# An attention and SwiGLU kernel: five of seven output products split once more, gate and value weights streamed

## The chip, the cores and the metric

The kernel runs on one core of a Trainium2 chip. The metric is the device time of one execution in microseconds. Four compute engines work beside each other: TensorE (PE, matrix products into PSUM), VectorE (DVE), ScalarE (ACT) and GpSimd (POOL); SyncE (SP) issues the transfers (DMAs) between HBM and the on-chip memory SBUF. Each engine runs its own instructions in a fixed order and waits on semaphores for the others.

## The reference

Attention over 8 batches of 8 heads, 576 tokens, head width 64, where scores more than `tau` below their row's maximum are dropped; then a SwiGLU feed-forward block over the 4608 tokens, all in float32:

```python
scores = scale * np.matmul(q, k.transpose(0, 1, 3, 2))
thresh = np.max(scores, axis=-1, keepdims=True) - tau
scores = np.where(scores >= thresh, scores, -1000000000.0)
...
attn = attn / (np.sum(attn, axis=-1, keepdims=True) + 1e-09)
attn_out = np.matmul(attn, v)
...
g = x @ w_gate                      # x: 4608 x 512, w_gate: 512 x 1536
silu = g * (1.0 / (1.0 + np.exp(-g)))
val = x @ w_val
return (silu * val @ w_out)         # w_out: 1536 x 512
```

## The kernel before

**The work.** A batch has four head pairs ("segments"), and each pair five slots: four tiles of 128 query tokens and a half tile of 64. So a batch has slots 0 to 19 (`kk`), and the half tiles are slots 4, 9, 14 and 19. A slot computes the scores of its tile (`slot_scores`, line 1155; PSUM tiles `sc`, two of them, each for 64 tokens and two heads), then the softmax (`slot_rest`, line 1181): row maxima on DVE, exponents on ACT, masks with row sums on DVE, an exchange of sums on ACT, the scaling by the reciprocal sum, half of it on GpSimd (line 1237) and half on ACT (line 1240), and a transpose on DVE (line 1241). One slot into the next segment, in slots 1, 6, 11 and 16, `attend` (line 1246) multiplies the segment's turned tiles by the values. It needs the transposes of all five slots.

**The feed-forward block of the batch before** runs in the same slots, for the first 512 tokens of each batch (a chunk `c`, here `c = b - 1`); the last 64 tokens of all batches form a ninth chunk. The products are by Winograd's form of Strassen's scheme: a product of 2 x 2 blocks by 7 block products instead of 8, with sums of blocks before and after.
- Gate and value: six groups of 256 columns per chunk, each with 7 products p1 to p7 of four matmuls 128x256 (class `Group`, line 878). Four of the seven weight operands lie in SBUF for good (`wgv`; one block is replaced by a difference, line 823). The three others are sums, stored once in HBM (`sums_hbm`) and loaded per group into a ring of two places, 768 KB each (`load_sums`, line 829).
- Output: class `Outputs` (line 1028) takes 256 tokens at a time, and so twice 7 products, each of six matmuls 128x256. Its results are added up in the tile `ob` by ACT copies and DVE additions with one operand in PSUM, and shipped by DMAs (`ship`, line 1079).

**What sets the order.** A class `Plan` collects jobs for DVE, ACT, POOL and SP, each with an estimated duration, the jobs it depends on and a rank, and puts them into each engine's order by when they can start. PE's order is written by hand: after a slot's scores come so many products of gate and value by the table `GV`, and so many output products by `CH` (`block_part`, line 1351):

```python
GV = {2: 4, 3: 3, 4: 3, 5: 4, 6: 1, 7: 4, 8: 3, 9: 3, 10: 3, 11: 2, 12: 4, 13: 4, 14: 3}
CH = {16: 1, 17: 3, 18: 2, 19: 2, 0: 3, 1: 1}
```

The output products of chunk c thus run from slot 15 to slot 1 of the next batch. After the last batch comes a tail (`tail[0] = True`): the last two chunks alone, without attention, with all sums of blocks on DVE.

Of the kernel before, what the change touches and what calls it, by code (L numbers as in the profile page):

```python
# [10 lines left out]
F32 = mybir.dt.float32  # L11
# [7 lines left out]
class Job:  # L19


    def __init__(self, eng, took, fn, rank, lag):
        self.eng, self.took, self.fn, self.rank, self.lag = eng, took, fn, rank, lag
        self.waits, self.ready, self.end, self.then = 0, 0.0, None, []


class Plan:
# [7 lines left out]
    def __init__(self):  # L35
        self.t = 0.0
        self.free = dict.fromkeys(("DVE", "ACT", "POOL", "SP"), 0.0)
        self.open = {e: [] for e in self.free}

    def job(self, eng, took, fn, *deps, rank=1, lag=0.0):  # L40
        j = Job(eng, took, fn, rank, lag)
        for d in deps:
            if isinstance(d, Job) and d.end is None:
                d.then.append(j)
                j.waits += 1
            elif d is not None:
                j.ready = max(j.ready, self.after(d, eng) if isinstance(d, Job) else d + self.HOP)
        if not j.waits:
            self.open[eng].append(j)
        return j  # L50
# [20 lines left out]
    def step(self):  # L71
        start, e, n = self.peek()
        j = self.open[e].pop(n)
        start = max(start, j.ready)
        j.fn()
        self.free[e] = start + j.took
        j.end = start + j.took + j.lag
        for k in j.then:
            k.waits -= 1
            k.ready = max(k.ready, self.after(j, k.eng))  # L80
            if not k.waits:
                self.open[k.eng].append(k)
# [26 lines left out]
def kernel(  # L109
# [64 lines left out]
    wgv = const.tile([P, 2, NCC, DFF], F32, name="wgv")  # L174
    wo = const.tile([P, 2, NF, DM2], F32, name="wo")
    extra = const.tile([P, 3 * WS], F32, name="extra")
    ring = const.tile([P, 2, 3 * HW], F32, name="ring")
# [4 lines left out]
    ob = const.tile([P, 2, DM], F32, name="ob")  # L182
    sums_hbm = hbm.tile([NF2, P, 3 * HW], F32, name="sums_hbm")
    last_hbm = hbm.tile([P, NCC, B * (S - SM)], F32, name="last_hbm")

    rall = ring.rearrange("p s n -> p (s n)")
# [46 lines left out]
    los = deque([extra[:, 4 * S + 2 * TW:], rall[:, 4 * S:], ob.rearrange("p i n -> p (i n)")[:, 0:TW]])  # L233
# [529 lines left out]

    def ring_part(s, n):
        return ring[:, s, n * HW:(n + 1) * HW].rearrange("p (k f) -> p k f", k=2)

# [47 lines left out]
    def weight_sums(g, place, *deps):  # L814
        t1, t2, t4 = (place[:, n * HW:(n + 1) * HW].rearrange("p (k f) -> p k f", k=2) for n in range(3))
        w11, w12, w21, w22 = pair_cols(wval, 0, g), pair_cols(wgat, 0, g), pair_cols(wval, 1, g), pair_cols(wgat, 1, g)
        j = job("POOL", 1.3, pool_tt(t1, w12, w11, ALU.subtract), *deps, rank=3)
        j = job("POOL", 1.3, pool_tt(t2, w22, t1, ALU.subtract), j, rank=3)
        j = job("POOL", 1.3, pool_tt(t4, w21, t2, ALU.subtract), j, rank=3)
        stores[g] = job("SP", 0.1, lambda: nc.sync.dma_start(out=sums_hbm[g], in_=place), j, lag=4.0)  # L820
        summed_g[g] = j
# [5 lines left out]
    loads = {}  # L827

    def load_sums(c, g, *deps):
        loads[c, g] = job("SP", 0.1, lambda: nc.sync.dma_start(out=ring[:, g % 2], in_=sums_hbm[g]), stores[g], *deps, lag=4.0)  # L830
# [47 lines left out]
    class Group:  # L878


        def __init__(self, c, g):
            self.c, self.g = c, g
            self.b = None

# [9 lines left out]
        def ring_w(self, n):  # L894
            return ring_part(self.g % 2, n)

# [5 lines left out]
        def p1(self, early=True):  # L902
            self.a = take("pa")
            self.m1 = self.mul(self.a, pair_cols(wval, 0, self.g), x_block(self.c, 0, 0), True, *self.a.deps, *ready_x[self.c][0])
            self.a.bank.full = True
            if early:
                self.take_b()

        def p5(self):
            self.take_b()  # L910
            self.e = take("pe")
            m = self.mul(self.e, self.ring_w(0), xs[0], True, loads[self.c, self.g], *ready_x[self.c][1], *self.e.deps)
            self.e.bank.full = True
            s, old = turn_of(s_bufs)
            self.s = s
            self.s5 = job("ACT", 0.55, lambda: nc.scalar.activation(s.ap, self.e.rows(), AF.Copy, scale=0.5), m, *old, rank=0)  # L916

        def p2(self):
            u, self.u1_old = turn_of(u_bufs)
            self.u1_buf = u  # L920
            if self.b is None:
                self.s1 = job("ACT", 0.55, lambda: nc.scalar.copy(u.ap, self.a.rows()), self.m1, *self.u1_old, rank=0)
                self.u1_old = []
            m = self.mul(self.a, pair_cols(wval, 1, self.g), x_block(self.c, 0, 1), False, self.cb if self.b else self.s1)
            self.m2 = m

        def p6(self):
            u = self.u1_buf
            if self.b:
                m = self.mul(self.b, self.ring_w(1), xs[1], False, self.cb, *ready_x[self.c][2])  # L930
            else:
                b = self.b = take("pb")
                m = self.mul(b, self.ring_w(1), xs[1], True, *ready_x[self.c][2], *b.deps)
                m = job("DVE", 0.7, lambda: nc.vector.tensor_tensor(out=b.rows(), in0=b.rows(), in1=u.ap, op=ALU.add),
                        m, self.s1, rank=0)
                b.bank.full = True
            self.u1 = job("ACT", 0.55, lambda: nc.scalar.activation(u.ap, self.b.rows(), AF.Copy, scale=0.5), m, *self.u1_old, rank=0)

# [14 lines left out]
        def p3(self):  # L953
            m = self.mul(self.e, pair_cols(wgat, 1, self.g), xs[2], False, self.s5, *ready_x[self.c][4])
            u = self.u1_buf
            g1 = job("DVE", 0.7, lambda: nc.vector.scalar_tensor_tensor(out=u.ap, in0=self.e.rows(), scalar=0.5, in1=u.ap, op0=ALU.mult,
                                                                        op1=ALU.add), m, self.u1, rank=0 if self.g == NF2 - 1 else 1)
            self.e.read_by(g1)
            self.e.done(True)
            self.finish(0, u, g1, self.a, self.m2)  # L960

        def p7(self):
            m = self.mul(self.b, pair_cols(wgat, 0, self.g), x_block(self.c, 1, 0), False, self.u1, parts[self.g], *ready_x[self.c][3])
# [7 lines left out]
        def p4(self):  # L971
            m = self.mul(self.b, self.ring_w(2), x_block(self.c, 1, 1), False, self.u2)
            self.finish(1, self.u2_buf, self.g2, self.b, m)
            if self.g + 2 < NF2:
                load_sums(self.c, self.g + 2, m)
# [52 lines left out]
    class Outputs:  # L1028
# [53 lines left out]
        def products(self):  # L1082
# [11 lines left out]
            def three():  # L1094
# [3 lines left out]
                z["s4"] = []  # L1098
# [27 lines left out]
    def outputs(c):  # L1126
# [10 lines left out]
        def run():  # L1137
            n, s, fn = steps.pop(0)
            fn()
            if s == 4:  # L1140
                mark = plan.t
                if n == 0:
                    units[1].half_sums(mark)
                elif c < B:
                    load_sums(c + 1, 0, mark)
                    if c == 0:
                        load_sums(1, 1, stores[NF2 - 1])
            return bool(steps)

        return first, run  # L1150

# [29 lines left out]
    def slot_rest(seg, t, pss, marks):  # L1181
# [53 lines left out]
        for x in range(m):  # L1235
            if x % 2 and t < NT:
# [51 lines left out]
    def prepare_next(i, later_than):  # L1288
# [10 lines left out]
        fj = job("SP", 0.8, fetch, later_than, lag=3.5)  # L1299
# [10 lines left out]
    def prepare_v(seg, *deps):  # L1310
        seg["vj"] = job("SP", 0.4, lambda: load_v(seg), *deps, lag=3.5)
# [9 lines left out]
    def gates_and_values(c):  # L1321

        old = None
        for g in range(NF2):
# [3 lines left out]
            if old is not None:  # L1328
                old.p4()
                yield  # L1330
            for fn in (new.p5, new.p2, new.p6, new.p3, new.p7):
                fn()
                yield
            old = new
        state["last_product"] = old.p4
# [10 lines left out]
    GV = {2: 4, 3: 3, 4: 3, 5: 4, 6: 1, 7: 4, 8: 3, 9: 3, 10: 3, 11: 2, 12: 4, 13: 4, 14: 3}  # L1346
    CH = {16: 1, 17: 3, 18: 2, 19: 2, 0: 3, 1: 1}
    PLAIN = {5: 2, 6: 0, 10: 2, 11: 0}
    CH0 = {14: 1, 15: 3, 16: 0, 17: 2, 18: 2, 19: 2, 20: 3, 21: 1}

    def block_part(b, kk):
# [13 lines left out]
        if kk in GV:  # L1365
            if kk == 2:
                state["gv"] = gates_and_values(c)
            gv_steps(GV[kk])
            if kk == 14:
                next(state["gv"], None)  # L1370
                first, state["run"] = outputs(c)
                first.half_sums()
        elif kk == 15:
            out_steps(1)
            state["last_product"]()
            load_sums(c + 1, 1, plan.t)
            out_steps(1)
        elif state["run"]:
            out_steps(CH.get(kk, 0))

    own = xall[:, 3 * XW:]
    WS = {8: (0, own), 9: (1, ring[:, 1]), 11: (2, own), 13: (3, ring[:, 1]), 15: (4, ring[:, 1]), 17: (5, ring[:, 1])}
    for n, seg in enumerate(halved):
        i = seg["i"]
        for x, t in enumerate(seg["tiles"]):
# [19 lines left out]
            slot_rest(seg, t, pss, marks)  # L1405
# [10 lines left out]
            if 18 <= s < 18 + 2 * NF2 and s % 2 == 0:  # L1416
                g = (s - 18) // 2
                weight_part(g, summed_g[g], plan.t)

    tail[0] = True  # L1420
    out_steps(3)
    attend(halved[-1])
    spare = []
# [14 lines left out]
    for c in (B - 1, B):  # L1438
        for _ in gates_and_values(c):
            pass  # L1440
        first, state["run"] = outputs(c)
        first.half_sums()
        out_steps(1)
        state["last_product"]()
        if c < B:
            load_sums(B, 1, plan.t)
# [42 lines left out]
```

## Time and profile before

| | |
|---|---|
| median of 3 runs | 1439.74 us (1439.49 to 1439.96) |
| the profiled execution | 1440.44 us, of which the span from first to last instruction is 1438.7 |
| granted TensorE clock | 0.998 of full speed |
| one batch (attend of slot 11 to the next) | 154.5 us |
| scores 128x288 exponent on ACT / mask on DVE | 495 / 510 ns |
| scaling of a tile on ACT / on POOL | 529 / 1012 ns |
| row maxima on DVE, per score tile | 747 ns |
| sum of 128x512 on POOL | 1275 ns |
| loads of weight sums | 48 of 768 KB, 4.5 us from issue to landing |

"PE" are matmuls and "PEld" the weight loads that run beside them. A float32 matmul leaves two records, so record counts are twice the number of matmuls. In the rows of groups the columns are the line, the engine, the operation, output and inputs with their tile names, the number of records, the busy time in us, and the mean of one in ns. A busy engine is not one that sets the time: that is seen from which wait ends last.

### The profile page before, as it was taken

How to read it: one execution, taken by the hardware profiler on the slowest of the kernel's cores; microseconds unless marked ns; L12 is line 12 of the kernel's file. 1: busy time of each engine (PE TensorE's matmuls, PEld its weight loads, DVE VectorE, ACT ScalarE, POOL GpSimd, SP SyncE). 2: the span in 40 equal slices, each digit the busy share in tenths (PEclk: the TensorE clock that was granted, in tenths of full speed). 3: DMA queues.
4: the chain of work that ended last, by engine and by line, in shares of the span. 5: the costliest groups of instructions: out<-in, count | busy, mean ns of one | idle time of the engine just before them, and what ended most of it. 6: DMA issues, size and time to landing. Idle time of an engine off the chain costs nothing.

```text
span 1438.7 us, 31145 instructions
## 1 busy us (share of the span) xinstructions
PE 1400.7 (97%) x11496; PEld 1078.7 (75%) x11496; DVE 1061.6 (74%) x3045; ACT 794.0 (55%) x2170; POOL 697.8 (49%) x686
## 2 busy tenths in 40 slices
PE   9999899999999999999999999999999999999998
PEld 6676666777777777777777777777777777888887
DVE  7988999888777878788788877887788874343343
ACT  6888765566646665566546664566556652220220
POOL 2465759965574448444754466445745462000000
PEclk9999999999999999999999999999999999999999
DMA  8734312353223312333232222332223311112101
GB/s 177 203 120 133 66 34 79 115 139 78 56 71 87 79 49 63 82 78 78 56 81 54 72 78 50 95 78 54 63 69 78 78 39 56 66 45 80 64 25 30
DMA packets 192071, 111.47 MB, mean 77 GB/s; under 512 B 165040, under 2 KB 166064, under 8 KB 191920
## 3 DMA queue, kind: packets, MB, share of 16 engines
q1 hardware_dynamic: 188320, 109.05, 28.5%
q8 instruction: 92, 1.51, 0.5%
q10 hardware_dynamic: 3600, 0.43, 0.2%
q14 instruction: 59, 0.48, 0.1%
HBM read 94.24 MB, written 15.20 MB: 76 GB/s over the span
## 4 chain that ended last, share of the span: by engine, by line
PE 76%; DVE 13%; ACT 6%; issue 2%; SPq 2%; DMA 1%; DVEq 0%; ACTq 0%
PE po L1054 22%; PE pb L890 14%; PE pa L890 10%; PE pe L890 10%; PE xa L1260 8%; PE sc L1173 7%; DVE pall L1210 3%; DVE mx L1195 2%; ACT pall L1209 2%; DVE pall L1241 1%; DVE mx L1201 1%; SPq L317 1%; DVE hall L944 1%; PE pv L498 1%; ACT sums L1224 1%
## 5 line engine op out<-in xcount | busy, mean ns | idle before, releaser
L1237 POOL TENSOR_SCALAR pall<-pall,ri 128x288 f32<-128x288 f32 x224 | 223.7, 1012 | 154.5 <-DVE ri L1230 153.4
L1210 DVE SCALAR_TENSOR_TENSOR pall<-sc,th,pall 128x288 f32<-128x288 f32 x504 | 233.1, 510 | 64.4 <-ACT pall L1209 63.3
L1209 ACT ACTIVATE pall<-sc,nm 128x288 f32<-128x288 f32 x504 | 213.6, 495 | 9.0 <-DVE pall L1210 9.0
L1195 DVE TENSOR_REDUCE mx<-sc 128x2 f32<-128x576 f32 x252 | 179.3, 747 | 38.2 <-PE sc L1173 37.2
L1054 PE MATMUL po<-wo,hall 128*128 128x256 f32 x852 | 196.2, 382 | 1.3 <-DVE hall L944 0.9
L1054 PEld LDWEIGHTS po<-wo,hall 128*128 128x128 f32 x852 | 159.6, 190 | 34.5 <-issue 5.8
L890 PE MATMUL pb<-xall,ring 128*128 128x256 f32 x768 | 184.5, 383 | 0.0
L890 PE MATMUL pa<-xall,wgv 128*128 128x256 f32 x768 | 183.3, 381 | 0.0
L1241 DVE STREAM_TRANSPOSE pall<-pall 128x1152 f32<-128x1152 f32 (+1 forms) x140 | 174.9, 1251 | 6.0 <-ACT pall L1240 3.5
L1205 ACT ACTIVATE th<-nm,cut 128x4 f32<-128x4 f32 (+1 forms) x140 | 41.5, 297 | 243.7 <-DVE nm L1202 219.6
L890 PEld LDWEIGHTS pb<-xall,ring 128*128 128x128 f32 x768 | 143.4, 190 | 31.9 <-issue 10.8
L1173 PE MATMUL sc<-kT,qT 64*32 64x288 f32 x4032 | 156.6, 410 | 9.1 <-DVE pall L1210 7.6
L890 PEld LDWEIGHTS pa<-xall,wgv 128*128 128x128 f32 x768 | 144.1, 190 | 27.6 <-ACT tmp L916 2.8
L768 POOL TENSOR_TENSOR hall<-hall,tmp 128x512 f32<-128x512 f32 x79 | 100.5, 1275 | 104.8 <-DVE hall L944 58.1
L1224 ACT COPY sums<-sums 32x4 f32<-32x4 f32 (+1 forms) x560 | 108.4, 194 | 74.7 <-DVE pall L1210 66.0
L1240 ACT ACTIVATE pall<-pall,ri 128x288 f32<-128x288 f32 x280 | 133.9, 529 | 26.6 <-DVE ri L1230 25.2
L1260 PE MATMUL xa<-pall,vall 64*64 64x288 f32 x2016 | 135.7, 409 | 12.3 <-DVE pall L1241 8.7
L1260 PEld LDWEIGHTS xa<-pall,vall 64*64 64x64 f32 x2016 | 88.4, 134 | 58.7 <-DVE pall L1241 12.0
L1173 PEld LDWEIGHTS sc<-kT,qT 64*32 64x32 f32 x4032 | 59.0, 105 | 79.2 <-issue 49.1
L1054 PE MATMUL po<-extra,ring 128*128 128x256 f32 x432 | 97.8, 382 | 0.6 <-DVE ob L1073 0.6
L1054 PEld LDWEIGHTS po<-extra,ring 128*128 128x128 f32 x432 | 80.9, 190 | 17.5 <-POOL hall L768 3.3
L890 PE MATMUL pe<-xall,ring 128*128 128x256 f32 x384 | 92.0, 382 | 0.0
(171 smaller groups left out, 2152.1 us busy)
## 6 DMA issues: line engine op xcount, KB each, us to landing
ring<-sums_hbm SPq DMA_DIRECT2D x48, 768.0 KB, 4.5
vall<-in_v_dram SPq DMA_DIRECT2D x112, 144.0 KB, 2.9
out_dram<-ob SPq DMA_DIRECT2D x32, 256.0 KB, 2.1
qT<-in_q_dram SPq DMA_DIRECT2D x112, 72.0 KB, 3.4
kT<-in_k_dram SPq DMA_DIRECT2D x112, 72.0 KB, 2.8
wo<-in_moe_w_gate_dram SPq DMA_DIRECT2D x16, 384.0 KB, 3.6
wo<-in_moe_w_val_dram SPq DMA_DIRECT2D x16, 384.0 KB, 4.1
sums_hbm<-ring SPq DMA_DIRECT2D x4, 768.0 KB, 4.2
```

The lines of the kernel that those rows point to most:

```text
L768: return lambda: nc.gpsimd.tensor_tensor(out=out, in0=a, in1=b, op=op)
L890: nc.tensor.matmul(ps[:, i], w[:, k_, i * P:(i + 1) * P], x[:, k_, :], start=first and i == k_ == 0, stop=True, skip_group_check=True)
L1054: nc.tensor.matmul(ps, h(f), w[:, f, :], start=(f == 0), stop=(f == NF2 - 1))
L1173: nc.tensor.matmul(ps[g * G:(g + 1) * G, h, 0:SH], qT[hs, col:col + G], kT[hs, c * SH:(c + 1) * SH], start=True, stop=True)
L1195: rs.append(job("DVE", 0.72, lambda x=x, tile_=tile_: nc.vector.tensor_reduce(out=mx[:, 2 * x:2 * x + 2, 0], in_=tile_[:, :, 0:SH], axis=A ...
L1209: ej = job("ACT", 0.42, lambda x=x: nc.scalar.activation(ps[x], scs[x], AF.Exp, bias=nm[:, x:x + 1]), ej, rank=0)
L1210: mj = job("DVE", 0.45, lambda x=x: nc.vector.scalar_tensor_tensor(out=ps[x], in0=scs[x], scalar=th[:, x:x + 1], in1=ps[x], op0=ALU.is_ge, ...
L1224: nc.scalar.copy(sm[g * G:(g + 1) * G, 0:m, 1], sm[o * G:(o + 1) * G, 0:m, 0])
L1237: scaled.append(job("POOL", 1.02, lambda x=x: nc.gpsimd.tensor_scalar(out=ps[x], in0=ps[x], scalar1=ri[:, x:x + 1], scalar2=None, op0=ALU. ...
L1240: scaled.append(job("ACT", 0.46, lambda x=x: nc.scalar.activation(ps[x], ps[x], AF.Copy, scale=ri[:, x:x + 1]), rj, rank=2))
L1241: seg["turned"].append(job("DVE", 0.72 * len(pss), lambda: nc.vector.transpose(out=whole, in_=whole), *scaled, rank=2 if t < NT else 1))
L1260: nc.tensor.matmul(holds[a].ap()[h * D:(h + 1) * D, 0:SH].rearrange("d (i q) -> d i q", q=G), vr[rs, h, j, :], p[rs, h, :, j, :], start=(j ...
```

## The change

Outputs of the chunks from 2 on (`DEEP = 2`, seven of nine) are made by a new class `Deep`. It takes 512 tokens at once with 7 outer products, so that each operand block is twice as large. Five of them (`NESTED`) are split once more into 7 inner products of three matmuls 128x128 (`nested`), with sums of quarter blocks before (`inner_sums`, on POOL, in the tail on DVE) and after (`combine`). The other two (`flat`) stay at twelve matmuls 128x256. The weight side of the inner sums is made once, in slots 2 to 6 of batch 3, over the place of `wgv` (`deepen`). Sums over outer products build up in PSUM: a product goes on adding to the same banks, and ACT copies the intermediate states out (`copies`). No VectorE sum with both inputs in SBUF is made before the tail.

For the same chunks all seven weight operands of gate and value are streamed: `store_plain` writes the four plain ones to HBM too, and `load_flow` loads each group in two parts of 1 MB and 0.75 MB into places that lie over `wgv` and the ring. `wgv`, the ring and `ob` are one tile.

In batches 3 to 7 the slots of a list (`BY_ACT`), 11 of the 16 with full tiles among them, have their scalings all on ACT, which moves 5 x 11 x 2 = 110 of them from POOL. The tables have changed: `GV` for all chunks, and for the new outputs `CD` (a product per step; `gates_end` is the chunk's last gate/value product). In slot 15 come p1 and `gates_end`, in 16 p2 and p5, then p6, p3, p7 and, in slot 0, p4. Planned durations of the q, k and v loads are longer, and the plan counts the time that a transfer takes (`moves`). Chunks 0 and 1 keep the old outputs and resident weights.

```diff
+    DEEP = 2
...
+    def load_flow(c, g, part, *deps):
+        lo, to = ((0, 4), (4, NQ))[part]
+        s = g % 2 * GW
+        loads[c, g, part] = job("SP", 0.1, lambda: nc.sync.dma_start(
+            out=flow[:, s + lo * HW:s + to * HW], in_=sums_hbm[g][:, lo * HW:to * HW]), stores[g], *plain_stores[g], *deps,
+                                  lag=1.6, moves=(3.8, 3.0)[part])
...
+    def deepen(o, *deps):
+        b11, b12, b21, b22 = quarters(operands[o])
+        t1, t2, t4 = (deeper_part(o, n) for n in range(3))
+        j = job("POOL", 1.0, pool_tt(t1, b12, b11, ALU.subtract), *deps, rank=3)
+        j = job("POOL", 1.0, pool_tt(t2, b22, t1, ALU.subtract), j, rank=3)
+        j = job("POOL", 1.0, pool_tt(t4, b21, t2, ALU.subtract), j, rank=3)
+        deep_jobs[o] = [job("POOL", 1.0, pool_tt(b12, b22, b12, ALU.subtract), j, rank=3)]
...
+        def nested(self, o, holds, first, *deps):
+
+            ws = weights_of(o)
+            begun = set() if first else {0, 1}
+            for n in self.ORDER:
+                a, ready = self.inner[o][n]
+                bank_, at_ = self.AT[n]
+
+                def fn(n=n, a=a, bank_=bank_, at_=at_):
+                    ps = holds[bank_].ap()[:, at_ * P:(at_ + 1) * P]
+                    for f in range(NF2 // 2):
+                        nc.tensor.matmul(ps, a[:, f, :], ws[n][:, f, :], start=bank_ not in begun, stop=True, skip_group_check=True)
+                        begun.add(bank_)
+
+                m = pe(0.655, fn, *ready, *deps, *deep_jobs[o])
+            return m
...
+        def combine(self, q, *deps, psum=False):
...
+            deps = *deps, *ob_jobs[n]
+            if psum:
+                one = y[:, free:free + 1]
+                deps = [job("ACT", 0.28, lambda: nc.scalar.copy(one, q0[:, 0:1]), *deps, rank=0)]
+                tt, eng, took, less, rank = dve_tt, "DVE", 0.42, 0.29, 0
+            else:
+                tt, eng, took, less, rank = (dve_tt, "DVE", 0.36, 0.23, 1) if tail[0] else (pool_tt, "POOL", 0.75, 0.44, 2)
+            twice = lambda x: x.broadcast_to((P, 2, P))
+            j = job(eng, took, tt(y[:, x:x + 2], twice(one), q0[:, 1:3], ALU.add), *deps, rank=rank)
+            j = job(eng, took, tt(y[:, x + 3:free + 1:free - x - 3], twice(y[:, x + 1:x + 2]), q1[:, 1:3], ALU.add), j, rank=rank)
+            j = job(eng, less, tt(y[:, x + 1], y[:, x + 3], q0[:, 3], ALU.add), j, rank=rank)
+            j = job(eng, took, tt(y[:, x + 2:x + 4], twice(y[:, free:free + 1]), q1[:, 0:2], ALU.add), j, rank=rank)
+            return n, j
...
+        def p4(self):
+            m = self.nested(3, self.x, False, *self.c7)
+            n, j = self.combine(self.x, m, psum=True)
+            self.done(self.x, j)
+            self.ship(1, 0, n, j)
...
+        def p4_alone(self):
+            x, deps = self.pair("px")
+            m = self.nested(3, x, True, *deps)
+            t = self.spaces
+            n, j = self.combine(t[1], *self.add(t[1], x, t[3], m, self.u3))
+            self.ship(1, 0, n, j)
...
-            if x % 2 and t < NT:
+            if x % 2 and t < NT and not by_act:
...
-    GV = {2: 4, 3: 3, 4: 3, 5: 4, 6: 1, 7: 4, 8: 3, 9: 3, 10: 3, 11: 2, 12: 4, 13: 4, 14: 3}
+    GV = {2: 3, 3: 4, 4: 2, 5: 5, 6: 1, 7: 3, 8: 2, 9: 3, 10: 5, 11: 2, 12: 3, 13: 3, 14: 5}
     CH = {16: 1, 17: 3, 18: 2, 19: 2, 0: 3, 1: 1}
+    BY_ACT = 0, 1, 4, 5, 6, 7, 9, 11, 12, 13, 14, 15, 16, 18
+    CD = {15: 2, 16: 2, 17: 1, 18: 1, 19: 1, 0: 1}
...
+        if state["run"] and c - (kk < 2) >= DEEP:
+            out_steps(CD.get(kk, 0))
...
-            slot_rest(seg, t, pss, marks)
+            slot_rest(seg, t, pss, marks, b > DEEP and kk in BY_ACT)
```

## Prediction

> **What bounds the kernel now.** I read the engine shares first, then the chain of waits, then what TensorE waits for, then 36-us windows of one period of the loop and of the end.
>
> ```profile
> PE 1400.7 (97%) x11496; PEld 1078.7 (75%) x11496; DVE 1061.6 (74%) x3045; ACT 794.0 (55%) x2170; POOL 697.8 (49%) x686
> ...
> PE 76%; DVE 13%; ACT 6%; issue 2%; SPq 2%; DMA 1%; DVEq 0%; ACTq 0%
> ```
>
> TensorE (PE) is busy nearly throughout and carries three quarters of the chain that ended last. So the time is PE's work plus the gaps that other engines leave in it. A change pays if it takes matmuls away and opens no new gap. From the waits of PE:
>
> ```profile
> PE xa L1260 <- DVE pall L1241: 8.7, 6, 1.5
> PE sc L1173 <- DVE pall L1210: 7.6, 10, 2.2
> ```
>
> (total us, times, longest). The first row repeats once per batch; on the timeline it is the attend of slot 11:
>
> ```profile
> 976.11 1.25 PE L1260 MATMUL xa<-pall,vall 64*64 64x288 f32 x14 [1.46 <-DVE pall L1241]
> ```
>
> The windows (PE, weight loads, DVE, ACT, POOL with counts, granted clock, DMA share, GB/s) show two stretches of the main loop and one of the tail:
>
> ```profile
> 972.00:1008.00 36.00, 34.54 (x328) 26.85 (x326) 28.24 (x85) 23.38 (x67) 19.58 (x20) 1.00 0.24 56
> 1008.00:1044.00 36.00, 35.84 (x314) 27.14 (x307) 28.23 (x91) 17.91 (x57) 27.08 (x32) 1.00 0.23 64
> 1224.00:1260.00 36.00, 36.00 (x168) 31.69 (x168) 12.16 (x18) 10.61 (x18) 0.00 (x0) 1.00 0.20 66
> ```
>
> The clock is full, so no part of the answer is a clock. VectorE (DVE) stands at 28 of 36 us in the main loop, the second busiest engine. The tail window holds nothing but PE: 168 records in 36.00 us. A matmul is two records, so a 128x256 matmul costs 2 x 36/168 = 0.43 us.
>
> **Matmuls removed and added.** The order of PE loses 420 matmuls of 128x256 (756 to 336) and gains 735 of 128x128: 35 nested products (5 in each of 7 chunks), each 21 small matmuls in place of 12 large ones. The rest of PE's work is unchanged. The old price is 420 x 0.432 = 181.4 us. For the new one the nearest row is the attention head's transposing by a plain matmul:
>
> ```profile
> 13.54 1.16 PE L452 MATMUL tp<-pall 128*128 128x128 f32 x8
> 14.63 0.43 PE L455 MATMUL end<-pall 128*64 128x128 f32 x2
> ...
> 65.69 1.09 PE L450 MATMUL tp<-pall 128*128 128x128 f32 x8
> 66.63 0.27 PE L457 MATMUL end<-pall 128*128 128x128 f32 x1
> ```
>
> Within the first group the records start every 0.112 us after the second; within the group at 65.69, true transposes, every 0.109; exactly half of the tail's pitch would be 0.107. I take 0.112, the same kind of instruction: 735 x 0.224 = 164.6 us, a **saving of 16.8 us**, 0.48 per product. At 0.107 it would be 24; with a 0.1-us gap at the head of each product (the first record of the group stands 0.21 before the second) 13.
>
> [...] The row decides: each of its records has its own load of 128 columns (191 ns in the groups, overlapped), and it still keeps 0.112. But it is 8 records long, and the new runs are 42.
>
> **Slot 1: a wait added.** A slot is one query tile's scores, then products from the hand-written tables. Attend of a finished head pair comes in slots 1, 6, 11 and 16 and needs DVE's transposes of all its tiles. Before, slot 1's attend has its cover:
>
> ```profile
> 895.12 0.77 DVE L1241 STREAM_TRANSPOSE pall<-pall 128x576 f32<-128x576 f32 x1
> ...
> 901.28 4.59 PE L1260 MATMUL xa<-pall,vall 64*64 64x288 f32 x72
> ```
>
> The half tile of slot 19 is turned 5.4 us before. Afterwards slot 0 ends in deep product p4, and on DVE this transpose stands behind the combine of p4, which waits for PE's end and an ACT copy. From p4's end: copy 0.3 with hand-over 0.5; four sums 0.42+0.42+0.29+0.42 = 1.55 (0.42 is the present `ob` sum of 128x256; 0.29 an estimate from it for half the width); transpose 0.77; hand-overs 0.3 to 0.5. That is 3.2 to 3.4 us, against slot 1's two score tiles of 1.13. The wait is 1.8 (if the hand-overs hide) to 2.8; I take 2.2, in batches 4 to 7: **+8.8**. Queued behind that transpose are slot 1's row maxima, and behind them ACT's exponents, but PE stands in attend (4.6) meanwhile.
>
> **Slots 8 to 11: one wait removed, one added.** Slot 10 goes from 3 gate/value products to 5, at 1.72 each, between the half tile's scores (slot 9) and attend in slot 11, so the 1.46 us there is covered by 3.4 us more work: it goes down to 0.2, six batches: **-7.8**. Slot 8 goes from 3 to 2 products, 3.44 us. The next scores need the PSUM tile that DVE's first two masks free: row maxima 1.42, exchange 0.63, minimum 0.16, threshold 0.30, exponent 0.50, two masks 0.88 = 3.9 bare, 5 as slots of the trace run. So scores of slot 9 wait 0.4 to 1.5; I take 0.7, six times: **+4.2**. It is bounded below by nothing.
>
> **The deep steps otherwise.** In slots 17 to 0 each deep product (4.7) or flat one (5.2) stands alone with its scores (1.13), so a slot lasts about 6; DVE needs 5.7 per full tile (1.42+0.63+0.16, masks 1.76, totals 0.33, transpose 1.38). From slot 17's scores to slot 1's attend I sum DVE at 22.6 us (with 1.5 for q/k transposes and 2.5 for sums of products) and PE at 24.4. It fits, barely. Missing output steps in slot 1 save one change of matmul shape, 0.2 x 4: **-0.8**.
>
> **Work off the path.** The copies of products on ScalarE, some 5 us per chunk, and 110 scalings of 0.53 moved to it from GpSimd raise it from 55% to some 65%. The moved scalings are neutral: a pair by each engine takes 1.99 on GpSimd, four on ACT 1.81. The nested operands are summed by GpSimd, about 30 us per chunk between p1 and p4, from which 22 scalings (22 us per batch) have gone; by the order each sum is ready some us ahead. If that cover goes, a product waits for one sum, 1.0 us (an estimate between 0.73 for 256 elements and 1.28 for 512). The 20 one-time weight sums at slots 2 to 6 of batch 3 add 20 us of GpSimd to a stretch with half of it idle: at most 0.5.
>
> SP streams all seven weight operands, 1.75 MB per group in two DMAs instead of 768 KB. The present load lands in 4.5 us, so the parts take some 6 and 4.5; they are asked for 17 us or more before use. SP issues 0.35 each, and the q/k loads queued behind are due a slot or more later: nothing, at most 0.5 a batch. In the tail attend now waits for one deep product's transposes, about 1.1 instead of 0.6, and the deep chunks there have small waits: **+1.0** with the weight sums.
>
> **The end.** Now PE's last matmul is followed by one sum and one output:
>
> ```profile
> 1428.87 5.34 PE L1054 MATMUL po<-wo,hall 128*128 128x256 f32 x24
> ...
> 1434.25 0.42 DVE L1073 TENSOR_TENSOR ob<-ob,po 128x256 f32<-128x256 f32 x1 [1.84 <-PE po L1054]
> ```
>
> Afterwards come sums of 0.69 and 0.55, the four of the combine (1.55), with hand-overs and the block's previous output 4.3 in all, then four output DMAs at about 0.5: last issue 5.8 after PE instead of 1.0: **+4.8**. Between +3 (no wait for the block) and +6.
>
> **Sum:** -16.8 +8.8 -7.8 +4.2 -0.8 +1.0 +4.8 = -6.6. The profiled execution took 1440.44 (span 1438.7 and 1.7 around it), which gives 1433.8; the median of the runs is 0.7 below it: **1433**.
>
> **Rivals.**
> - *The waits do not come.* The combine finishes early enough, slot 8's masks hold no one: 1433 - 8.8 - 4.2 = **1420**. For it: PE's gaps are now under 2 us in 154, and an order with slots of two products keeps its score tiles fed elsewhere. Against it: the transpose stands behind the combine in DVE's fixed order. Chance 0.30.
> - *VectorE becomes the bound of slots 17 to 1* (the slower side). PE has 24.4 us there and DVE 22.6. If each of DVE's handovers adds 0.2 to some 25 operations, DVE needs 27.6 and attend in slot 1 waits 3 us longer, 5.2 in four batches, and slots of c=2 another 1: 1433 + 12 + 1 = **1446**. It turns the sign from 3.85 us per batch (6.6/4 more than 2.2). For it: DVE at 28 of 36 already; against: those 28 include transposes that could run later. Chance 0.20, a part of which ends within the bound.
> - *Weight loads set the pace of 128 columns*: [...] Against it the 0.112 row. Chance 0.02.
> - *The streamed weights hold up q/k or arrive late*: twice the bytes, a queue in order. At 3 us a batch for 5 batches, **1448**, at 1 us 1438; the DMA share of 0.24 speaks against it. Chance 0.03.
>
> That the change does not do what it says is excluded by the order: the 735 small matmuls are there.
>
> **Numbers.** The forecast has 0.45, with its own range 1427 to 1439. About 0.2% (2.9 us, 1436.9 to 1442.6) is what cannot be told from no change. Faster: 0.41 of the forecast, 0.30, and 0.01 of the late loads, 0.72. Same: 0.04 + 0.08 of VectorE + 0.01 = 0.13. Slower: 0.12 + 0.02 + 0.01 = 0.15. The range runs from the first rival with a little of the 0.107 pitch, 1419, to 1442.
>
> **What would show it.** Pitch of the 128x128 records inside deep products, 0.112; a gap before attend in slot 1 of batches 4 to 7, released by DVE's transpose, near 2.2; no 1.46 gap in slot 11; a gap of under 1.5 before scores of slot 9; last DMA issue some 5.8 after the last matmul. The forecast fails if the small records come at 0.13 or more, or if scores in slots 17 to 0 wait for masks in every batch.

## The result, and the profile after

| | before | after |
|---|---|---|
| median, us (4 runs each) | 1439.62 | 1430.80 |
| range of the runs | 1439.33 to 1439.96 | 1429.78 to 1431.63 |
| span of the profiled execution | 1438.7 | 1429.8 |

The ratio is 0.9938, 95% interval 0.9921 to 0.9956. The change makes the kernel faster by 8.8 us; the forecast was 1433 with a range of 1419 to 1442.

The page of the changed kernel, engine shares and the chain that ended last:

```profile
PE 1383.1 (97%) x12126; PEld 1080.7 (76%) x12126; DVE 1083.8 (76%) x3063; ACT 863.5 (60%) x2319; POOL 721.4 (50%) x672
...
PE 74%; DVE 14%; ACT 4%; POOL 3%; issue 2%; DMA 2%; SPq 1%; ACTq 0%; DVEq 0%; POOLq 0%
```

PE is still the bound, with 17.6 us less busy time (1400.7 to 1383.1). The span fell by only half of that, 8.9. The rest went into waits (some 5 us more in all) and the end (3.4 us more). What PE waited for:

```profile
PE sc L1513 <- DVE pall L1550: 16.2, 25, 2.1
PE xa L1600 <- issue: 6.4, 4, 1.6
...
PE px L1305 <- ACT tmp L1325: 0.7, 1, 0.7
```

The row of attend behind DVE's transposes with 8.7 us is gone, but attend has a new one with 4 x 1.6 us, and scores wait for masks 25 times instead of 10. A deep product waits only once. The place of the new waits, batch 6, on the timeline of PE:

```profile
897.91 0.83 PE L1305 MATMUL px<-extra,hall 128*128 128x128 f32 x6
898.67 1.30 PE L1513 MATMUL sc<-kT,qT 64*32 64x288 f32 x32
901.58 4.83 PE L1600 MATMUL xa<-pall,vall 64*64 64x288 f32 x72 [1.60 <-issue]
906.49 0.72 PE L1513 MATMUL sc<-kT,qT 64*32 64x288 f32 x16
907.72 0.72 PE L1513 MATMUL sc<-kT,qT 64*32 64x288 f32 x16 [0.50 <-DVE pall L1550]
```

and at the same time on DVE:

```profile
899.13 1.65 DVE L795 TENSOR_TENSOR big<-big,px 128x256 f32<-128x256 f32 x4
900.71 0.77 DVE L1581 STREAM_TRANSPOSE pall<-pall 128x576 f32<-128x576 f32 x1
```

The first line is p4's combine, the second the half tile's transpose, which ends 0.1 us before attend begins. The profile names "issue" as releaser; the order on DVE points to the cause, and a run below tests it. Slot 11's attend now follows its scores without a gap:

```profile
666.21 1.20 PE L1513 MATMUL sc<-kT,qT 64*32 64x288 f32 x32
667.34 0.96 PE L1600 MATMUL xa<-pall,vall 64*64 64x288 f32 x12
```

How far the changed kernel is behind (+) or ahead (-) at certain points, from the starts of attend and the last matmul in both traces:

| point | before | after | difference |
|---|---|---|---|
| batch 2, slot 1 | 284.02 | 284.56 | +0.5 |
| batch 2, slot 6 | 321.47 | 324.80 | +3.3 |
| batch 3, slot 11 | 512.59 | 514.23 | +1.6 |
| batch 7, slot 11 | 1130.58 | 1126.72 | -3.9 |
| attend in the tail | 1208.62 | 1204.55 | -4.1 |
| last matmul ends | 1434.21 | 1422.00 | -12.2 |
| end of the span | 1438.7 | 1429.8 | -8.9 |

The gain has two sources, then: the main loop, 1.4 us per batch from batch 3 on after a loss of 3 us in batch 2, and the tail. Of the 8.1 us between attend in the tail and the last matmul, 2.6 are one old output step that used to stand behind this attend and now has no counterpart there; 5.5 are the tail's own.

### The profile page after: what moved, and what is told of

Read it like the earlier page. It is cut to its first block, busy times and chain, and to the rows that moved or that the text cites. A ratio compares the mean times of both kernels' runs of the same rounds, so it can differ in the third digit from the quotient of the medians.

```text
span 1429.8 us, 32622 instructions
## 1 busy us (share of the span) xinstructions
PE 1383.1 (97%) x12126; PEld 1080.7 (76%) x12126; DVE 1083.8 (76%) x3063; ACT 863.5 (60%) x2319; POOL 721.4 (50%) x672
## 4 chain that ended last, share of the span: by engine, by line
PE 74%; DVE 14%; ACT 4%; POOL 3%; issue 2%; DMA 2%; SPq 1%; ACTq 0%; DVEq 0%; POOLq 0%
PE pb L937 15%; PE px L1305 11%; PE pa L937 10%; PE pe L937 10%; PE sc L1513 8%; PE xa L1600 6%; PE py L1317 5%; PE po L1103 4%; DVE pall L1550 3%; DVE mx L1535 3%; PE sc L937 2%; DVE pall L1581 2%; ACT pall L1549 2%; DVE mx L1541 1%; DVE pall L429 1%
## 5 line engine op out<-in xcount | busy, mean ns | idle before, releaser
L937 PE MATMUL pb<-xall,big 128*128 128x256 f32 x1032 | 247.0, 382 | 0.0
L937 PEld LDWEIGHTS pb<-xall,big 128*128 128x128 f32 x1032 | 193.0, 190 | 38.6 <-issue 5.6
L1580 ACT ACTIVATE pall<-pall,ri 128x288 f32<-128x288 f32 x390 | 183.9, 530 | 21.8 <-DVE ri L1570 20.6
L937 PE MATMUL pa<-xall,big 128*128 128x256 f32 x752 | 180.9, 383 | 0.0
L937 PE MATMUL pe<-xall,big 128*128 128x256 f32 x752 | 179.6, 382 | 0.4 <-DVE hall L990 0.4
L1513 PE MATMUL sc<-kT,qT 64*32 64x288 f32 x4032 | 160.9, 410 | 19.6 <-DVE pall L1550 16.2
L937 PEld LDWEIGHTS pa<-xall,big 128*128 128x128 f32 x752 | 140.3, 190 | 32.0 <-ACT tmp L960 7.4
L1577 POOL TENSOR_SCALAR pall<-pall,ri 128x288 f32<-128x288 f32 x114 | 115.1, 1021 | 96.3 <-DVE ri L1570 95.8
L937 PEld LDWEIGHTS pe<-xall,big 128*128 128x128 f32 x752 | 141.3, 190 | 27.6 <-issue 5.6
L1541 DVE TENSOR_REDUCE mx<-mx 32x4 f32<-32x4 f32 (+1 forms) x560 | 83.1, 148 | 10.4
L989 ACT ACTIVATE vall<-tmp 128x512 f32<-128x512 f32 x96 | 60.4, 633 | 31.7 <-DVE tmp L1002 29.0
```

What stands on the lines that cost most here:

```text
L937: nc.tensor.matmul(ps[:, i], w[:, k_, i * P:(i + 1) * P], x[:, k_, :], start=first and i == k_ == 0, stop=True, skip_group_check=True)
L1513: nc.tensor.matmul(ps[g * G:(g + 1) * G, h, 0:SH], qT[hs, col:col + G], kT[hs, c * SH:(c + 1) * SH], start=True, stop=True)
L1577: scaled.append(job("POOL", 1.02, lambda x=x: nc.gpsimd.tensor_scalar(out=ps[x], in0=ps[x], scalar1=ri[:, x:x + 1], scalar2=None, op0=ALU. ...
L1580: scaled.append(job("ACT", 0.46, lambda x=x: nc.scalar.activation(ps[x], ps[x], AF.Copy, scale=ri[:, x:x + 1]), rj, rank=2))
```

## The experiments

Each of the twelve runs was timed beside the kernel before on the same chip. There were three such chips, where the kernel before took 1440.68 (the first four runs below), 1439.09 and 1439.36 us (the last four), so runs are best compared by their ratios; "period" is the time from attend in slot 11 of batch 6 to that of batch 7 in the trace (154.5 before, 153.1 after).

| run | median, us | ratio to before (interval) | period |
|---|---|---|---|
| changed kernel | 1430.8 | 0.9938 (0.9921 to 0.9956) | 153.1 |
| combine of p4 later | 1428.4 | 0.9914 (0.9899 to 0.9929) | 152.2 |
| changed, old table | 1438.2 | 0.9988 (0.9982 to 0.9995) | 155.3 |
| before, new table | 1434.8 | 0.9958 (0.9943 to 0.9973) | 153.3 |
| 5 deep chunks | 1431.8 | 0.9940 (0.9925 to 0.9955) | 153.1 |
| no scalings moved | 1459.3 | 1.0135 (1.0119 to 1.0150) | 159.5 |
| p4 before p3 in the tail | 1432.0 | 0.9952 (0.9939 to 0.9966) | 153.3 |
| slot 8 with 3, slot 10 with 4 | 1448.5 | 1.0071 (1.0057 to 1.0084) | 157.7 |
| four edits together | 1442.5 | 1.0019 (1.0011 to 1.0027) | 155.1 |
| end on two queues | 1431.2 | 0.9936 (0.9921 to 0.9951) | 153.1 |
| three edits together | 1422.5 | 0.9878 (0.9862 to 0.9894) | 152.3 |
| each streamed load twice | 1542.7 | 1.0709 (1.0686 to 1.0732) | 175.3 |
| before, new table, scalings moved | 1439.7 | 0.9997 (0.9988 to 1.0005) | 154.4 |

**The table and the deep outputs taken apart.** Three runs: the changed kernel with the old `GV`, the kernel before with the new one, and the deep outputs begun at chunk 4, with the scalings on ScalarE still from batch 3 on.

```diff
-    GV = {2: 3, 3: 4, 4: 2, 5: 5, 6: 1, 7: 3, 8: 2, 9: 3, 10: 5, 11: 2, 12: 3, 13: 3, 14: 5}
+    GV = {2: 4, 3: 3, 4: 3, 5: 4, 6: 1, 7: 4, 8: 3, 9: 3, 10: 3, 11: 2, 12: 4, 13: 4, 14: 3}
```

> The changed kernel with the old table GV for all chunks. If the table removed the gaps, those before attend in slot 11 (1.46) and slot 6 (0.31) return in six batches, +10, slot 9's scores wait no more, -3, and what batch 2 lost at its start (about 3 us) comes back: 1434 to 1439. Rival, the smaller products are the whole gain and the table is nothing: 1429.5 to 1432.

> The kernel before with the new table GV and nothing else. If the gaps of slots 11 and 6 are the table's: -9 to -11 for six batches, +3 for slot 9's scores, +2 to 3 for batch 2: 1434 to 1437. Rival, the new table pays only together with the new outputs: 1438 to 1442.

```diff
-    DEEP = 2
+    DEEP = 4
...
-                elif c == 0:
-                    load_sums(1, 0, mark)
-                    load_sums(1, 1, stores[NF2 - 1])
+                elif c + 1 < DEEP:
+                    load_sums(c + 1, 0, mark)
+                    if c == 0:
+                        load_sums(1, 1, stores[NF2 - 1])
...
+            if c + 1 < DEEP:
+                load_sums(c + 1, 1, plan.t)
...
-            slot_rest(seg, t, pss, marks, b > DEEP and kk in BY_ACT)
+            slot_rest(seg, t, pss, marks, b > 2 and kk in BY_ACT)
```

> Two-level outputs and streamed weights from chunk 4 on instead of 2: 5 chunks instead of 7, so 10 nested products fewer; GV and the scalings on ScalarE as in the changed kernel. PE's work rises by 10 x 0.48 = 4.8 us. If a deep chunk of the main loop gives its 2.4 us back in waits of slots 1 to 3 (1.6 + 0.5 + 0.4), the time stays within 1429.5 to 1432.5. Rival, these waits are not the deep chunks': +4 to 5, 1435 to 1436.

With the old table slot 11 has a gap again (1.10 instead of 1.46, and the profile names ScalarE as releaser instead of DVE), and slot 4 gets one of its own. From that run:

```profile
930.62 1.56 PE L937 MATMUL pa<-xall,big 128*128 128x256 f32 x6 [1.24 <-ACT pb L944]
...
978.12 1.15 PE L1600 MATMUL xa<-pall,vall 64*64 64x288 f32 x8 [1.10 <-ACT vall L989]
```

Its period of 155.3 is longer than the 154.5 of the kernel before: with the old table the deep outputs cost time in the main loop. The new table alone does 153.3 without any deep product, and 1434.8 in all, 5.9 us of the 8.8 (as a difference to the kernel before timed beside it, 1440.68). With 5 deep chunks the time is the same as with 7 within the runs (1430.2 to 1434.6), and its two batches with old outputs took 153.1 and 152.9 (attend in slot 11, batches 3 to 4 and 4 to 5), against 153.1 of its deep ones.

The three runs agree: **against the best batches with old outputs, the deep outputs of this order save next to nothing in the main loop.** Their waits give back what PE saves: in the period PE waits 1.60, 0.50, 0.37 and 0.52 us in the changed kernel, 3.0 in all, against 0.22 and 0.94, 1.2 in all, with the new table alone; without the waits the two periods are 150.1 and 152.1. The table is what gains in the main loop, and the deep outputs gain in the tail: from attend in the tail to the last matmul the changed kernel takes 217.4 us and the new table alone 225.9, of which 2.6 are the step that moved. The split is not sharp, since the intervals of the two ratios overlap (0.9958 and 0.9938), and one run below (the kernel before with the new table and the moved scalings, period 154.4) is a worse old order, beside which the deep outputs would look better by 1.3 us.

**The wait of slot 1.** The combine of p4 loses its precedence on DVE (rank 1 instead of 0).

```diff
-        def combine(self, q, *deps, psum=False):
+        def combine(self, q, *deps, psum=False, last=False):
...
-                tt, eng, took, less, rank = dve_tt, "DVE", 0.42, 0.29, 0
+                tt, eng, took, less, rank = dve_tt, "DVE", 0.42, 0.29, 1 if last else 0
...
             m = self.nested(3, self.x, False, *self.c7)
-            n, j = self.combine(self.x, m, psum=True)
+            n, j = self.combine(self.x, m, psum=True, last=True)
```

> Only the combine after outer product p4 in the main loop loses its precedence (rank 1 instead of 0), so that on VectorE the half tile's transpose stands ahead of it. If the 1.6 us gap before attend in slot 1 of batches 4 to 7 is due to that place in the order alone, it goes (to 0.3 or less) and the time falls by 4 to 6 us from 1430.8, to 1425 to 1427. Rival, VectorE as the bound of slots 17 to 3: the same sums are still to be made, the wait moves to the scores of slots 2 and 3, and the time stays within 1429.5 to 1432.

```profile
1049.49 1.30 PE L1513 MATMUL sc<-kT,qT 64*32 64x288 f32 x32
1050.72 4.76 PE L1600 MATMUL xa<-pall,vall 64*64 64x288 f32 x72
...
1063.99 0.72 PE L1513 MATMUL sc<-kT,qT 64*32 64x288 f32 x16 [0.94 <-DVE pall L1550]
```

Attend now follows at once, so the place in DVE's order was the cause. But slot 3's scores wait 0.94 (0.37 before the edit) and slot 5's 0.70. The period is 0.9 shorter, of waits of 2.5 us in slots 1 to 3, and the median of 1428.4 lies above the first answer's 1425 to 1427 and below the rival's 1429.5: both hold in part. The sums that remain take DVE's time a little later.

**The scalings on ScalarE.** `BY_ACT` switched off in the changed kernel, and put into the kernel before together with the new table.

```diff
-            slot_rest(seg, t, pss, marks, b > DEEP and kk in BY_ACT)
+            slot_rest(seg, t, pss, marks, False)
```

> The changed kernel with no scalings moved from GpSimd to ScalarE. The forecast costed the move at nothing: 1430 to 1432. Rival from the gaps seen since (before slot 9's scores 0.52 with the move, 0.94 with the new table alone; slot 11's 1.10 against 1.46): the move hands DVE its transposes earlier and is worth 0.5 to 0.8 in each of five batches, 1433 to 1435. A third, GpSimd's sums for the deep chunks come late without the move and PE waits for them at products px: above 1435.

> The kernel before with the new table GV and the changed kernel's scalings on ScalarE, old outputs, resident weights. By the batches of the run with 5 deep chunks that still had old outputs, a batch takes 152.9 us, 0.4 less than with the new table alone: 1431.5 to 1433.5, so that the deep outputs bring only 1 to 2 us. Rival, the scalings only help where GpSimd makes the deep sums: 1434.5 to 1435.5.

Without the move the time is 1459, 28 us worse and slower than the kernel before. PE in slot 16 of batch 5, and GpSimd beside it:

```profile
880.44 1.50 PE L1305 MATMUL px<-big,hall 128*128 128x128 f32 x12
884.93 0.94 PE L1305 MATMUL px<-wo,hall 128*128 128x128 f32 x6 [2.99 <-POOL hall L792]
```

```profile
877.62 1.01 POOL L792 TENSOR_TENSOR hall<-hall 128x384 f32<-128x384 f32 x1
878.58 2.91 POOL L792 TENSOR_TENSOR xall<-xall 128x256 f32<-128x256 f32 x4
881.45 1.26 POOL L792 TENSOR_TENSOR hall<-hall 128x512 f32<-128x512 f32 x1
882.66 1.26 POOL L792 TENSOR_TENSOR big<-hall,big 128x512 f32<-128x512 f32 x1
883.88 0.99 POOL L792 TENSOR_TENSOR hall<-hall 128x384 f32<-128x384 f32 x1
884.85 1.98 POOL L1577 TENSOR_SCALAR pall<-pall,ri 128x288 f32<-128x288 f32 x2
```

GpSimd works without a pause, and the last inner sum of product p2 (128x384, ending 884.87) comes 3 us late. Five such waits make 15 us; the rest are longer waits for masks (20.5 us instead of 16.2) and slower matmuls: the same 12126 records of PE take 1393.7 us instead of 1383.1, some of them at half the clock (the last section). In the kernel before, with the new table, the same move makes things worse by some 5 us (1434.8 to 1439.7; ratios 0.9958 and 0.9997), so both answers on record for this run missed. The timeline shows ACT's copies of attend in slot 6 among the exponents there, and slot 7's scores waiting 0.81. So the move is worth nothing by itself: it pays for room on GpSimd. In the run with 5 deep chunks batches with old outputs were better off (152.9) with the same two edits. There ACT makes slot 7's four exponents in one piece before attend's copies, and slot 7's scores do not wait; that kernel plans with other durations for the loads. Whether these durations are what gave the better order was not tried.

**Slots 8 and 10.**

```diff
-    GV = {2: 3, 3: 4, 4: 2, 5: 5, 6: 1, 7: 3, 8: 2, 9: 3, 10: 5, 11: 2, 12: 3, 13: 3, 14: 5}
+    GV = {2: 3, 3: 4, 4: 2, 5: 5, 6: 1, 7: 3, 8: 3, 9: 3, 10: 4, 11: 2, 12: 3, 13: 3, 14: 5}
```

> In the table GV slot 8 has 3 products instead of 2 and slot 10 has 4 instead of 5. If slot 9's scores wait (0.52) only because slot 8 is short, that gap goes in six batches, and with 4 products slot 10 still covers slot 11's attend: 1427.5 to 1428.5. Rival: slot 10 needs its fifth product, attend in slot 11 waits about 1 us again, and the time is 1430.5 to 1434.

Neither. Slot 9's scores do not wait any more, but the product after the next does:

```profile
964.60 1.99 PE L937 MATMUL pb<-xall,big 128*128 128x256 f32 x8
969.66 3.78 PE L937 MATMUL pe<-xall,big 128*128 128x256 f32 x8 [3.07 <-DVE hall L990]
```

It needs a PSUM bank that DVE's sum of `hall` frees, and DVE runs that one at 968.96, after slot 9's masks. In batches 3, 5, 6 and 7 this costs 3.1 us each, 12 in all. After the one shown matmuls run at half speed for a while (the last section), and over the whole run the same 12126 records of PE take 1390.3 us instead of 1383.1, 7.2 more. The order of products decides which bank is free when, and one product moved by two slots costs 18 us.

**The end.** In the tail p4 made before p3; and, in another run, half of the last eight transfers issued by ScalarE.

```diff
-                self.steps = deque([self.p1, self.gates_end, self.p2, self.p7_alone, self.p5, self.p6_alone, self.p3, self.p4_alone])
+                self.steps = deque([self.p1, self.gates_end, self.p2, self.p7_alone, self.p5, self.p6_alone, self.p4_alone, self.p3])
```

> In the tail the nested product p4 is made before the flat product p3, so that what follows TensorE's last matmul is one sum of 128x512 and four transfers, not two sums and a combine that waits for transfers of its block. From the last matmul to the end falls from 7.8 to about 5.5 us: 1428 to 1429.5. Rival: the four transfers' issues, which queue behind eight others, set the end, and the swap brings under 1 us: 1430 to 1431.

```diff
-                            nc.sync.dma_start(out=out[r:r + D, cols], in_=o[x * D:(x + 1) * D, i])
+                            q = nc.scalar if x and (t, e) in ((0, 1), (1, 0)) else nc.sync
+                            q.dma_start(out=out[r:r + D, cols], in_=o[x * D:(x + 1) * D, i])
```

> The last two blocks of the ninth chunk are shipped by two transfers issued by SyncE and two by ScalarE each, instead of four by SyncE. The twelve last issues on SyncE take 9.6 us in the changed kernel, 0.8 each, and end 5.3 us after TensorE's last matmul. If this queue sets the end, the time from the last matmul to the end falls from 7.8 by 2 to 3 us: 1428 to 1429. Rival, the sums and the combine after the last matmul set it: 1430.5 to 1431.5.

In the first of these the combine of p4 writes over the block to which p3 still adds, so one quarter of the outputs of the last two chunks is wrong, and its time stands for no usable kernel. From the last matmul to the end it took 9.8 us instead of 7.8: the one sum behind the last matmul waits for transfers of its block. The second cut the 7.8 to 6.8, less than the 2 to 3 us expected, and the median did not move (1431.2); a gain of 1 us is within the spread of these runs. First the changed kernel's last twelve issues, and the last four of them alone, then those of the kernel with two queues, SP and ACT:

```profile
1417.68 9.64 SPq L1367 DMA_DIRECT2D out_dram<-big  x12
```

```profile
1424.94 2.38 SPq L1367 DMA_DIRECT2D out_dram<-big  x4
```

```profile
1418.04 7.77 SPq L1368 DMA_DIRECT2D out_dram<-big  x8
```

```profile
1418.65 7.43 ACTq L1368 DMA_DIRECT2D out_dram<-big  x4
```

The long stretches hold a wait: the first eight issues of the changed kernel start 0.6 apart and are over at 1422.6, and SP then stands until the last combine at 1424.9. After the last matmul (1422.0) the sums and this combine take 2.9 us, the last four issues 2.4 and the landing of the last transfer 2.5. With two queues these are 2.3, 1.4 and 3.0. So both answers name a part of the end.

**The streamed loads.** Each is issued twice, in one step, with the order on all compute engines unchanged.

```diff
-        loads[c, g, part] = job("SP", 0.1, lambda: nc.sync.dma_start(
-            out=flow[:, s + lo * HW:s + to * HW], in_=sums_hbm[g][:, lo * HW:to * HW]), stores[g], *plain_stores[g], *deps,
+        loads[c, g, part] = job("SP", 0.1, lambda: [nc.sync.dma_start(
+            out=flow[:, s + lo * HW:s + to * HW], in_=sums_hbm[g][:, lo * HW:to * HW]) for _ in range(2)], stores[g], *plain_stores[g], *deps,
```

> Each streamed load of gate and value weights is issued twice in a row, so 3.5 MB per group instead of 1.75; all compute instructions stand in the same order. If the stream is hidden with room to spare, the time stays within 1430 to 1432.5. Rival, the queue is near its limit: q, k, v or weights come late, above 1436.

1542.7, but not for want of bandwidth: the loads land in 5.1 and 4.8 us, as before (5.3 and 4.9). The second load waits on SP for the first (85 such waits of 5.5 us in the mean), and so holds the queue. SP, then DVE, in batch 4:

```profile
580.38 20.83 SPq L870 DMA_DIRECT2D big<-sums_hbm  x6
601.30 0.39 SPq L1362 DMA_DIRECT2D out_dram<-big  x1
```

```profile
606.22 1.65 DVE L795 TENSOR_TENSOR big<-big,px 128x256 f32<-128x256 f32 x4 [7.48 <-DMA out_dram<-big]
607.78 0.77 DVE L1581 STREAM_TRANSPOSE pall<-pall 128x576 f32<-128x576 f32 x1
```

An output transfer stands behind the loads; the combine waits for it to leave the block; the half tile's transpose stands behind the combine; and attend waits 9 us. So the run says little about the stream's bytes and much about SP's queue: in the changed kernel the same transfer is issued at 583.10, 18 us earlier.

**Together.** The first attempt took the combine's rank, the swapped tail (with the block written over as above), slots 8 and 10, and the old products in slots 2 to 5 of batch 2 (the diff below). The second left out the swapped tail and slots 8 and 10 and took the two queues at the end.

```diff
-            gv_steps(GV[kk])
+            gv_steps({2: 4, 3: 3, 4: 3, 5: 4}.get(kk, GV[kk]) if b == 2 else GV[kk])
```

> Four edits together: combine of p4 at rank 1, p4 before p3 in the tail, slots 8 and 10 with 3 and 4 products, and the old 4, 3, 3, 4 products for slots 2 to 5 of batch 2 alone, where the changed kernel lost about 3 us. If they are separate places: 1430.8 - 2.4 - 2 - 3 - 2.5 = 1421. If VectorE is so full that the wait only moves, 1425 to 1428.

> The changed kernel with three edits: combine of p4 at rank 1, the old 4, 3, 3, 4 products in slots 2 to 5 of batch 2 alone, and the last transfers on two queues. From 1430.8: 2.4 for the first (its run), about 2.5 for the second (what the attend of slot 1 of batch 2 came earlier with the old table), 2 to 3 for the third: 1423 to 1425. Rival: the gain of batch 2 is lost again by its slot 11, 1425 to 1427.

The first gave 1442.5, with the 3.1-us gaps of slots 8 and 10 in it. The second gave 1422.5, ratio 0.9878: 17 us below the kernel before and 8 below the change, a little better than the 1423 to 1425 expected. Attend in slot 6 of batch 2 (the expectation calls it slot 1) came at 322.58 instead of 324.80, and in slot 11 of batch 7 the run stood 6.2 us ahead of the changed kernel. So part of what the deep outputs lose in waits can be won back by the order: the period of 152.3 is 1.0 below that of the new table alone.

## Why the prediction was right, point by point

The sign and size were right (-6.6 forecast, -8.8 measured), and most terms were near; two were missing, and one "nothing" was wrong. That the sum came out so near is in part luck: the misses below come to some 9 us one way and 11 the other.

- *Small matmuls* (-16.8 forecast). Inside a deep product the records come every 0.112 us, as the row of `tp` said, and over 42 records too, each with its own weight load of 192 ns beside it; the rival in which the loads set the pace did not come. But the first record takes 0.1 more in most of the main loop's products (12 records take 1.60 us at the head of one at 893.79 and 1.50 further on, at 896.57), so one costs 4.79 there, not 4.70. That makes 25 x 0.39 + 10 x 0.49 = 14.7.
- *Slot 1* (+8.8): 1.60 instead of 2.2, four times, 6.4, a little under the lower bound of 1.8. The hand-overs hid: DVE goes from slot 0's masks to the combine at 899.13, 0.4 after p4's last record. What was not costed is behind it: DVE is late for slots 2 and 3, 0.50 and 0.37, another 3.5. The rival with VectorE as the bound was right about the place and too large in the price.
- *Slot 11* (-7.8): the 1.46 went altogether, 8.8, and 0.31 of slot 6 in five batches, 1.6, which was not forecast. The run with the new table alone confirms this as the main gain.
- *Slot 6's attend* (not forecast; "the rest of PE's work is unchanged"). Before, its third pair of records came 1.0 us after the first, of which the profile counts 0.31 as idle and 0.7 as busy. The kernel before in batch 6, then the changed one:

```profile
938.72 0.70 PE L1260 MATMUL xa<-pall,vall 64*64 64x288 f32 x4
939.73 4.58 PE L1260 MATMUL xa<-pall,vall 64*64 64x288 f32 x68 [0.31 <-DVE hall L944]
```

```profile
938.14 4.60 PE L1600 MATMUL xa<-pall,vall 64*64 64x288 f32 x72
```

From its first record to the next product it took 5.5 us and takes 4.5. In five batches the hidden 0.7 makes 3.5. It is the table's too: with the new table alone PE's busy time falls from 1400.7 to 1397.1.

- *Slot 9* (+4.2): 0.52 in five batches and 1.16 in batch 2, 3.8.
- *The start* (not forecast): +3 in batch 2, mostly slot 3's scores (1.41) and a product of slot 4 (0.44). Neither the old table with deep outputs nor the new table alone has the first; it takes three products in slot 2 together with the changed kernel's order, in which DVE's transpose waits for GpSimd.
- *The end* (+4.8): 7.8 from the last matmul instead of 4.5, +3.4, within the +3 to +6 given.
- *Scalings* ("neutral"): wrong as a price. The comparison of 1.99 us on one engine with 1.81 on the other missed that they stand ahead of the deep sums in GpSimd's queue. The forecast's price "if that cover goes" was one sum, 1.0; without the cover it is 3.0 per batch in one place and 28 us in all. So the list of moved slots, which the forecast set at nothing, is a condition of the gain.
- *Streamed loads* (nothing): right for the changed kernel, where no wait of PE names them.
- *The tail's waits* (+1.0): one of 0.68 where there was one of 0.61, so nothing. (The prediction's tail window is not PE alone, as it says: DVE and ACT work in it too. The pitch read from it holds.)

These terms sum to -8.5 (-14.7 + 6.4 + 3.5 - 8.8 - 1.6 - 3.5 + 3.8 + 3 + 3.4); the traces show -8.9. What the forecast had wrong is the share of the new products: in the main loop it gave them some -4 (25 x 0.48 = 12 saved, 8.8 of waits, 0.8 of shape changes), and the runs show about nothing (9.8 saved, 6.4 + 3.5 of waits), while the table brought slot 6 beside its slot 11. The 0.8 of shape changes, an estimate of 0.2 for each, was not taken apart; what the trace before shows is that 24 records of `po` in a row took 5.38 us (at 416.19) and 36 took 7.97 (at 407.09), so 2.59 for 12 more, and 12 alone between attend and scores 2.79 (at 403.18).

## What to carry to other kernels

Fewer matmul columns are only worth what the engine that finishes each product leaves of them: here 2 us saved per batch were given back by VectorE within four slots. Where an order is written by hand, test the table apart from the algorithm; the table alone made some two thirds of this gain. And a sum placed at the head of a vector queue should be checked against what stands behind it, not only against what it releases.

## What the runs showed of the hardware

Some gaps of 2 to 3 us in PE's work were followed by half the granted clock, and others of the same length were not. Windows of 3.41 us (PE, weight loads, DVE, ACT, POOL, clock, DMA share, GB/s) show both: first a gap of 3.07 us in the run with slots 8 and 10 changed, then another of 3.08 in that run, then one of 2.27 in the changed kernel:

```profile
965.37:968.78 3.41, 1.22 (x6) 0.74 (x4) 2.58 (x12) 2.78 (x8) 1.27 (x1) 1.00 0.34 74
968.78:972.20 3.42, 2.54 (x6) 2.07 (x7) 3.27 (x7) 2.52 (x8) 2.99 (x3) 0.50 1.18 263
972.20:975.61 3.41, 3.41 (x9) 2.66 (x9) 1.18 (x2) 1.02 (x2) 0.24 (x1) 0.50 0.46 67
975.61:979.02 3.41, 3.41 (x43) 2.23 (x43) 1.89 (x6) 0.00 (x0) 0.00 (x0) 1.00 0.03 5
```

```profile
497.75:501.16 3.41, 1.65 (x8) 1.11 (x6) 2.57 (x10) 2.76 (x7) 1.27 (x1) 1.00 0.24 34
501.16:504.57 3.41, 2.09 (x10) 1.86 (x11) 3.25 (x9) 2.94 (x10) 2.55 (x3) 1.00 1.11 284
```

```profile
66.47:69.88 3.41, 1.14 (x7) 0.71 (x6) 3.08 (x7) 2.58 (x7) 1.68 (x1) 1.00 0.75 214
69.88:73.29 3.41, 3.41 (x10) 2.69 (x9) 3.15 (x8) 3.41 (x7) 2.27 (x2) 0.50 0.04 16
```

In the first, the clock stands at 0.50 from 968.78 to 975.61; a product of 8 records takes 3.78 us instead of 1.89 and the next one 3.07, so some 3 us are lost on top of the gap. After the second the clock stayed at 1.00, from 504 to 508 too. The third was followed by 0.50 for 3.41 us, and by 1.00 from 73.29 on. The run without the moved scalings has both cases as well: PE stood idle for 2.85 us of the 4 from 564 to 568, and the clock was 0.70 in the next 4 us and 0.87 in the 4 after them; about the gap of 2.99 us that ends at 884.93 it was 1.00 from 880 to 900. So a gap cost its own length in some places, and in the one counted here another 3 us. What decides between the two was not shown.
